# Attention into two expert layers: zero matmuls at the start, two weight loads and some small copies moved to other engines

## The chip, the cores and the metric

One core of one Trainium2 chip runs the program. It has TensorE (PE, with its weight loads as PEld), VectorE (DVE), ScalarE (ACT), GpSimd (POOL) and the sync engine (SP), which issues most DMAs. The metric is device time in microseconds, the median of several executions.

## The reference

Three stages follow each other on 2304 tokens (4 batches of 576) of width 512. The first is attention over a sliding window of 64 positions, 8 heads of 64. The second is a dense layer with a rational function between its two matrix products. The third sends each token to one of 8 experts.

```
scores = scale * q @ k.T ; mask: 0 <= row - col < 64, else -1e9
attn = exp(scores - max) ; attn /= sum(attn) + 1e-9 ; x = attn @ v
h = x @ w_in ; P = a0 + a1 h + a2 h^2 + a3 h^3
Q = 1 + |b0| |h| + |b1| h^2 ; y = (P / (Q + 1e-6)) @ w_out
e = argmax(y @ w_gate) ; weight = softmax(y @ w_gate)[e] * sigmoid(y @ w_output_gate)[e]
out = weight * (relu(y @ w1[e]) @ w2[e])
```

## The kernel before

Tokens go in 9 blocks of 256 (`TB`), and attention in 36 units: a block and a pair of heads each. For unit n, `at_T` transposes k and q on TensorE (line 308) and evacuates them to `kT` and the block-diagonal `qbd` (lines 157 to 163); from the second block on it first copies the last 64 columns of `kT` to its front (line 311 on GpSimd or 313 on VectorE, whichever is less charged). `at_QK` multiplies them into `sc`, takes the row minima of the negated, masked scores on VectorE (line 343), exponentials with row sums `sg` on ScalarE (349), adds 1e-9 to the sums on VectorE (352), takes reciprocals (353) and multiplies (`ms*sg`, line 173, on VectorE or GpSimd). `at_PT` transposes the weights, `at_PV` multiplies by v and splits the result into `xh` and `xl`.

q, k and v come through the sync queue in `load_qk` and `load_v`. For the first two blocks `load_v` loads each v row once and makes the shifted arrangement by three copies on chip (`copy`, line 167 on ScalarE or 169 on VectorE): one of 64 partitions and 512 numbers, two of 64 and 256.

The weights of the dense layer arrive as 64-bit floats. `load_w` loads a block of 1 MB, `convert` makes two fp32r halves of it: three integer operations of VectorE on each half block (288, 290, 292), a cast (167 or 169) and a subtraction (173). `c_conv(n)` starts conversions up to number n and issues the loads ahead of them.

The order of each engine's work is set when the kernel is built: the scheduler takes instructions by priority, which is program order shifted by `later(...)`, as its own timing model finds them ready, and each engine then runs its list in order. `evac`, `copy`, `arith` and `pick` give an operation to the engine whose charged load (`load`, by the formulas in `dve`, `act` and `pool`) would be lowest; `charge` adds the load of operations with a fixed engine. Ahead of the dense layer's first step, `PRE_E` = 12 half events of attention are emitted with `PRE_C` = 8 conversions among them, the first after `C_OFF` = 3 events; after that a step s emits the two products of one slice of 256 of the 2048 hidden columns, with attention and conversions paced beside it.

Of the kernel before, what the change touches and what calls it, by code (L numbers as in the profile page):

```python
# [1 line left out]

# [25 lines left out]
NG, HF = 3, 4  # L28
C_AT = ((-1, PRE_C), (6, 16), (15, 28), (18, 32))
A_OFF = 14  # L30
C_OFF, PREP = 3, 6
P_C, P_A, P_Y, P_L, P_E, P_G, P_S = -30, 0, -30, 0, 30, -30, 60
RK_R, G_LAG, F_LAG, F_LD, TR_S = 5, 3, 0, 1, 71

# [2 lines left out]
def kernel(  # L37
# [21 lines left out]
    W = 64  # L59
# [85 lines left out]
    def dve(n, fast=False):  # L145
        return 0.07 + n / (1920.0 if fast else 960.0)
# [84 lines left out]
    def load_v(m):  # L231
        u, g = divmod(m, 2)
        t = t4([128, 4, 4, D], "v")
        if u < VU:
            for x in range(2):
                for off, n, b, s in runs(u * TB + x * 128, 128):
                    nc.sync.dma_start(out=t[off:off + n, 2 * x + 1],
                                      in_=v[b, 4 * g:4 * g + 4, s:s + n, :].rearrange("h p d -> p h d"))
            copy(t[W:, 0:4:2], t[:W, 1:4:2], 8 * D)
            copy(t[:W, 2], t[W:, 1], 4 * D)  # L240
            copy(t[:W, 0], v_t[m - 2][W:, 3] if u else t[:W, 1], 4 * D)
            v_t[m] = t
            return
        for i in range(4):
            b, bi = divmod(4 * u + i, BPS)
            s0 = max(bi - 1, 0) * W
            n = W if bi == 0 else 2 * W
            nc.sync.dma_start(out=t[:n, i], in_=v[b, 4 * g:4 * g + 4, s0:s0 + n, :].rearrange("h p d -> p h d"))
        v_t[m] = t
# [6 lines left out]
    pos = {jf: s for s, jf in reversed(list(enumerate(seq)))}  # L256
    ffirst = [pos[0, fp] for fp in range(NFP)]

    def load_w(n):
        kind, fp = cseq[n]  # L260
        if kind == 0:
            t = t8([128, KD, 512], "stg", U32)
            src = w_in_u[:, fp * 512:(fp + 1) * 512]
        else:
            t = t8([128, 2, 1024], "stg", U32)
            src = w_out_u[fp * 256:(fp + 1) * 256, :]
        nc.sync.dma_start(out=t, in_=src.rearrange("(k p) f -> p k f", p=128))
        for i in range(2):
            r = t[:, 2 * i:2 * i + 2, :] if kind == 0 else t[:, i, :]
            stg[kind, fp, i] = (r[:, :, 0::2], r[:, :, 1::2]) if kind == 0 else (r[:, 0::2], r[:, 1::2])  # L270

    def convert(c):
# [7 lines left out]
        else:  # L280
            if i == 0:
# [3 lines left out]
        t = t2(shp, "ct")  # L285
        pu = pt(shp, "cp").bitcast(U32)
        charge("D", 2.0)
        nc.vector.tensor_scalar(out=pu, in0=hi, scalar1=3, scalar2=0x3FFFFFF8,
                                op0=ALU.logical_shift_left, op1=ALU.bitwise_and)
        nc.vector.scalar_tensor_tensor(out=pu, in0=hi, scalar=0xC0000000, in1=pu,  # L290
                                       op0=ALU.bitwise_and, op1=ALU.bitwise_or)
        nc.vector.scalar_tensor_tensor(out=t.bitcast(U32), in0=lo, scalar=29, in1=pu,
# [5 lines left out]


    P_t, pT_t, x_t = {}, {}, {}  # L300

    def at_T(n):
        u, c = divmod(n, NP)
        tq = pt([128, 2, 2, 128], "tq")
        cc = 2 * (c % 2)
        for a, src in ((0, k_t[n // 2]), (1, q_t[n // 2])):
            for r in range(2):
                nc.tensor.transpose(tq[:, a, r, :], src[:, r, cc:cc + 2, :].rearrange("p h d -> p (h d)"), ident)
        if u:
            if pick(D=dve(W, True), A=act(W), P=0.2) == "P":  # L310
                nc.gpsimd.tensor_copy(out=kT[c][:, :W], in_=kT[c][:, TB:])
            else:
                nc.vector.tensor_copy(out=kT[c][:, :W], in_=kT[c][:, TB:])
        evac(kT[c][:, W:], tq[:, 0].rearrange("d r p -> d (r p)"), TB)
        for hh in range(2):
            lo = 64 * hh
            evac(qbd[n % NQ][lo:lo + 64, :, lo:lo + 64],
                 tq[lo:lo + 64, 1].rearrange("d r (b p) -> d (r b) p", b=2), 256, -scale)
# [10 lines left out]
    def at_QK(n):  # L329
# [10 lines left out]
            nk.append(w)  # L340
        for i in range(4):
            charge("D", dve(128))
            nc.vector.tensor_tensor_reduce(
                out=ms[:, i, :nk[i]], in0=sc[:, i, :nk[i]], in1=cs[:, C_MASK + 128 - nk[i]:C_MASK + 128],
                scale=1.0, scalar=3.0e38, op0=ALU.add, op1=ALU.min, accum_out=mn[:, i:i + 1],
            )
        for i in range(4):
            charge("A", act(128))
            nc.scalar.activation(out=ms[:, i, :nk[i]], in_=ms[:, i, :nk[i]], func=AF.Exp,
                                 scale=-1.0, bias=mn[:, i:i + 1], accum_out=sg[:, i:i + 1])  # L350
        charge("D", 0.2)
        nc.vector.tensor_scalar(out=sg, in0=sg, scalar1=1e-9, scalar2=None, op0=ALU.add)
        nc.vector.reciprocal(out=sg, in_=sg)  # L353
        for a, b, w in spans(nk):
            arith(ms[:, a:b, :w], ms[:, a:b, :w], bc(sg[:, a:b], [128, b - a, w]), ALU.mult, (b - a) * w)
        P_t[n] = (ms, nk)

    def at_PT(n):
        ms, nk = P_t.pop(n)
# [514 lines left out]


    nc.vector.memset(one, 1.0)
    nc.scalar.preload_act_table_set("natural_log_exp_and_others")
    cseq.extend((kind, f0 + fp) for f0 in range(0, NFP, HF) for kind in range(2) for fp in range(HF))
    cpos = [0, 0]
# [78 lines left out]
    nc.sync.dma_start(out=cs, in_=cst[:, :C_TRI])  # L958
    v_upto(0)
    qk_upto(1)  # L960
    c_load(1)
    for t in qbd:
        nc.gpsimd.memset(t, 0.0)
    nc.scalar.activation(out=co[:, 4:6], in_=co[:, 4:6], func=AF.Abs)

    def prepare():
        wgs = t2([128, KD, 2 * E], "wgs")
# [52 lines left out]

    for n in range(TA):
        at_T(n)
    for i in range(PRE_E):
        at_upto(i + 1)
        c_conv(max(0, PRE_C * (i + 1 - C_OFF) // (PRE_E - C_OFF)))

    last = {j: s for s, (j, fp) in enumerate(seq) if fp == NFP - 1}
# [134 lines left out]
```

## Time and profile before

| | us |
|---|---|
| median of 3 runs | 808.82 (808.23 to 809.24) |
| the profiled execution | 810.46 |
| its span, first to last instruction | 808.5 |
| TensorE busy | 766.3 (95%) |
| VectorE busy | 539.0 (67%) |
| ScalarE busy | 506.3 (63%) |
| GpSimd busy | 449.9 (56%) |

Busy shares are means over stages that have different limits. Idle time counts where the engine that idles is the one that its stage waits for. A matmul's duration in a row is from issue to its modelled end, and the matmuls overlap; the busy time of a group, over its count, is the time from one to the next.

### The profile page before, as it was taken

Reading aid. Unit: us, or ns where it says so; the run is one execution under the profiler, and the core shown is the slowest. Engines: PE = TensorE matmul, PEld = TensorE weight load, DVE = VectorE, ACT = ScalarE, POOL = GpSimd, SP = SyncE. Lnnn points to the kernel's source line nnn. Section 1 sums busy time; section 2 is a strip of 40 time slices with the busy share of each in tenths; the row PEclk is TensorE's granted clock in tenths of the full one; section 3 lists DMA queues with packets and bytes.
Section 4 is the critical chain, followed back from the end, with each engine's and each line's share of the span. In section 5 each row is a group of like instructions: output and inputs, shape, how many; then the busy total and the mean of one; then the engine's idle time right before and its main releaser. Section 6 shows DMA issues by size and latency. Waiting matters only on the chain. (4 is left out here: it accounts for less than half of the span.)

```text
span 808.5 us, 15245 instructions
## 1 busy us (share of the span) xinstructions
PE 766.3 (95%) x5456; PEld 690.8 (85%) x5456; DVE 539.0 (67%) x1289; ACT 506.3 (63%) x1122; POOL 449.9 (56%) x399
## 2 busy tenths in 40 slices
PE   5868999999999999999999999897998999999994
PEld 4758899888899899999999998786997999999993
DVE  5799999876776766666676667465655456654630
ACT  5889786997766686676676665673525555543420
POOL 2596786665555555565654654675523554556430
PEclk9999999999999999999999999998998999999997
DMA  9786351422321211112120000323618777767610
GB/s 227 223 234 180 92 183 79 131 77 57 84 67 27 51 54 37 41 53 53 27 67 14 1 27 1 101 84 97 243 50 328 273 234 213 239 228 257 212 55 14
DMA packets 105602, 95.26 MB, mean 118 GB/s; under 512 B 77424, under 2 KB 77808, under 8 KB 105520
## 3 DMA queue, kind: packets, MB, share of 16 engines
q1 hardware_dynamic: 101840, 84.49, 35.1%
q0 software_dynamic: 3680, 9.73, 3.2%
q8 instruction: 45, 0.74, 0.4%
q14 instruction: 37, 0.30, 0.1%
HBM read 83.02 MB, written 11.44 MB: 117 GB/s over the span
## 5 line engine op out<-in xcount | busy, mean ns | idle before, releaser
L178 PE MATMUL y<-wo,g 128*128 128x512 f32 x864 | 220.1, 402 | 4.3 <-POOL g L173 3.3
L178 PE MATMUL h<-xh,wi 128*128 128x256 f32 x1024 | 195.8, 284 | 0.0
L178 PEld LDWEIGHTS y<-wo,g 128*128 128x128 f32 x864 | 158.4, 191 | 35.8 <-POOL g L173 3.5
L178 PEld LDWEIGHTS h<-xh,wi 128*128 128x128 f32 x1024 | 164.4, 192 | 2.7 <-DVE xl L388 0.2
L178 PE MATMUL h<-xl,wi 128*128 128x256 f32 x512 | 145.9, 285 | 0.0
L173 POOL TENSOR_TENSOR wx<-wr,wx 128x1024 fp32r<-128x1024 f32 x31 | 83.6, 2707 | 59.8 <-ACT wx L167 51.2
L173 POOL TENSOR_TENSOR g<-t,g 128x512 fp32r<-128x512 f32 x72 | 93.0, 1294 | 40.1 <-ACT g L167 34.8
L178 PE MATMUL hp<-xdh,wx 128*128 128x256 f32 x576 | 109.9, 290 | 3.8 <-ACT xdh L786 3.7
L173 POOL TENSOR_TENSOR qm<-qm,e 128x512 f32<-128x512 f32 x72 | 93.4, 1297 | 35.7 <-ACT qm L420 32.2
L178 PE MATMUL yp<-wx,hT 128*128 128x512 f32 x432 | 101.9, 392 | 0.0
L178 PEld LDWEIGHTS h<-xl,wi 128*128 128x128 f32 x512 | 98.3, 192 | 2.5
L178 PEld LDWEIGHTS hp<-xdh,wx 128*128 128x128 f32 x576 | 93.9, 198 | 5.3 <-ACT xdh L786 4.2
L415 ACT ACTIVATE e<-h 128x512 f32<-128x512 f32 x72 | 43.0, 597 | 87.3 <-PE h L178 87.1
L178 PEld LDWEIGHTS yp<-wx,hT 128*128 128x128 f32 x432 | 80.0, 188 | 16.4 <-DVE hT L794 0.3
L173 DVE TENSOR_TENSOR wx<-wr,wx 128x1024 fp32r<-128x1024 f32 x45 | 69.1, 1545 | 26.0 <-ACT wx L167 25.7
L167 ACT CAST wx<-wr 128x1024 fp32r<-128x1024 f32 x68 | 69.2, 1046 | 27.1 <-DMA wr<-in_moe_w_dram 21.8
L178 PE MATMUL hp<-xdl,wx 128*128 128x256 f32 x288 | 83.1, 290 | 0.7 <-DVE xdl L787 0.7
L440 DVE SCALAR_TENSOR_TENSOR t<-t,KK,r 128x512 f32<-128x512 f32 x72 | 53.6, 744 | 41.0 <-ACT r L434 40.6
L422 POOL TENSOR_SCALAR qm<-e,KK 128x512 f32<-128x512 f32 x45 | 34.6, 768 | 49.4 <-ACT e L415 49.2
L426 DVE TENSOR_TENSOR t<-t,h 128x512 f32<-128x512 f32 x72 | 49.1, 681 | 17.1 <-ACT t L416 17.0
L173 POOL TENSOR_TENSOR ms<-ms,sg 128x512 f32<-128x512 f32 (+4 forms) x60 | 39.2, 669 | 37.0 <-DVE sg L353 19.7
L433 ACT ACTIVATE r<-qm,KK 128x512 f32<-128x512 f32 x72 | 49.5, 688 | 15.3 <-POOL qm L173 14.7
(169 smaller groups left out, 1399.3 us busy)
## 6 DMA issues: line engine op xcount, KB each, us to landing
wr<-in_moe_w_dram SPq DMA_DIRECT2D x80, 512.0 KB, 4.8
stg<-in_moe_w_in_dram SPq DMA_DIRECT2D x8, 1024.0 KB, 6.7
stg<-in_moe_w_out_dram SPq DMA_DIRECT2D x8, 1024.0 KB, 7.4
v<-in_v_dram SPq DMA_DIRECT2D x58, 128.0 KB, 2.8
q<-in_q_dram SPq DMA_DIRECT2D x32, 128.0 KB, 2.8
k<-in_k_dram SPq DMA_DIRECT2D x32, 128.0 KB, 2.9
y_dram<-ysb SPq DMA_DIRECT2D x12, 256.0 KB, 2.1
yp_dram<-yq SPq DMA_DIRECT2D x6, 256.0 KB, 2.6
```

The costliest lines, as they stand in the source:

```text
L167: nc.scalar.copy(out=o, in_=i)
L173: (nc.vector if e == "D" else nc.gpsimd).tensor_tensor(out=o, in0=a, in1=b, op=op)
L178: pe[0] = nc.tensor.matmul(o, lhsT, rhs, start=start, stop=stop).ins
L415: nc.scalar.activation(out=e, in_=h, func=AF.Abs)
L422: (nc.vector if ef == "D" else nc.gpsimd).tensor_scalar(out=qm, in0=e, scalar1=co[:, 5:6], scalar2=co[:, 4:5], op0=ALU.mult, op1=ALU.add)
L426: nc.vector.tensor_tensor(out=t1, in0=t1, in1=h, op=ALU.mult)
L433: nc.scalar.activation(out=r0, in_=qm_t[s], func=AF.Ln, bias=qc_col)
L440: nc.vector.scalar_tensor_tensor(out=t1, in0=t1, scalar=co[:, 0:1], in1=r0, op0=ALU.add, op1=ALU.mult)
```

## The change

`at_T` and the start: a tile `wz` of zeros is set by VectorE, and `warm(n)` multiplies it n times by `one` into a PSUM tile that nothing reads: ten times at the start, six times behind the transposes of unit 1, six times behind those of the newest unit when four events are emitted. The first two weight blocks are loaded in two halves each by ScalarE's queue, behind its first activation (`Abs`), instead of by the sync queue. `C_OFF` becomes 0, and the first operation of each of the first four conversions is kept behind the newest unit's last row minimum on VectorE. The three copies in `load_v`, the `kT` copy in `at_T` and the addition of 1e-9 to `sg` are put on GpSimd, with loads charged for them.

```diff
--- before.py
+++ after.py
@@ -1,4 +1,4 @@
-from contextlib import ExitStack, contextmanager
+from contextlib import ExitStack, contextmanager, nullcontext
 
 import concourse.bass as bass
 import concourse.tile as tile
@@ -28,7 +28,7 @@
 NG, HF = 3, 4
 C_AT = ((-1, PRE_C), (6, 16), (15, 28), (18, 32))
 A_OFF = 14
-C_OFF, PREP = 3, 6
+C_OFF, PREP = 0, 6
 P_C, P_A, P_Y, P_L, P_E, P_G, P_S = -30, 0, -30, 0, 30, -30, 60
 RK_R, G_LAG, F_LAG, F_LD, TR_S = 5, 3, 0, 1, 71
 
@@ -236,9 +236,10 @@
                 for off, n, b, s in runs(u * TB + x * 128, 128):
                     nc.sync.dma_start(out=t[off:off + n, 2 * x + 1],
                                       in_=v[b, 4 * g:4 * g + 4, s:s + n, :].rearrange("h p d -> p h d"))
-            copy(t[W:, 0:4:2], t[:W, 1:4:2], 8 * D)
-            copy(t[:W, 2], t[W:, 1], 4 * D)
-            copy(t[:W, 0], v_t[m - 2][W:, 3] if u else t[:W, 1], 4 * D)
+            for o, i in ((t[:W, 0], v_t[m - 2][W:, 3] if u else t[:W, 1]), (t[W:, 0:4:2], t[:W, 1:4:2]),
+                         (t[:W, 2], t[W:, 1])):
+                charge("P", 0.6)
+                nc.gpsimd.tensor_copy(out=o, in_=i)
             v_t[m] = t
             return
         for i in range(4):
@@ -256,7 +257,7 @@
     pos = {jf: s for s, jf in reversed(list(enumerate(seq)))}
     ffirst = [pos[0, fp] for fp in range(NFP)]
 
-    def load_w(n):
+    def load_w(n, eng=None):
         kind, fp = cseq[n]
         if kind == 0:
             t = t8([128, KD, 512], "stg", U32)
@@ -264,7 +265,13 @@
         else:
             t = t8([128, 2, 1024], "stg", U32)
             src = w_out_u[fp * 256:(fp + 1) * 256, :]
-        nc.sync.dma_start(out=t, in_=src.rearrange("(k p) f -> p k f", p=128))
+        src = src.rearrange("(k p) f -> p k f", p=128)
+        if eng is None:
+            nc.sync.dma_start(out=t, in_=src)
+        else:
+            h = t.shape[1] // 2
+            for i in range(2):
+                eng.dma_start(out=t[:, i * h:(i + 1) * h], in_=src[:, i * h:(i + 1) * h])
         for i in range(2):
             r = t[:, 2 * i:2 * i + 2, :] if kind == 0 else t[:, i, :]
             stg[kind, fp, i] = (r[:, :, 0::2], r[:, :, 1::2]) if kind == 0 else (r[:, 0::2], r[:, 1::2])
@@ -285,8 +292,9 @@
         t = t2(shp, "ct")
         pu = pt(shp, "cp").bitcast(U32)
         charge("D", 2.0)
-        nc.vector.tensor_scalar(out=pu, in0=hi, scalar1=3, scalar2=0x3FFFFFF8,
-                                op0=ALU.logical_shift_left, op1=ALU.bitwise_and)
+        with tc.issue_after(dl[0]) if cpos[1] < 4 else nullcontext():
+            nc.vector.tensor_scalar(out=pu, in0=hi, scalar1=3, scalar2=0x3FFFFFF8,
+                                    op0=ALU.logical_shift_left, op1=ALU.bitwise_and)
         nc.vector.scalar_tensor_tensor(out=pu, in0=hi, scalar=0xC0000000, in1=pu,
                                        op0=ALU.bitwise_and, op1=ALU.bitwise_or)
         nc.vector.scalar_tensor_tensor(out=t.bitcast(U32), in0=lo, scalar=29, in1=pu,
@@ -298,6 +306,7 @@
 
 
     P_t, pT_t, x_t = {}, {}, {}
+    pl, dl = [None], [None]
 
     def at_T(n):
         u, c = divmod(n, NP)
@@ -305,12 +314,10 @@
         cc = 2 * (c % 2)
         for a, src in ((0, k_t[n // 2]), (1, q_t[n // 2])):
             for r in range(2):
-                nc.tensor.transpose(tq[:, a, r, :], src[:, r, cc:cc + 2, :].rearrange("p h d -> p (h d)"), ident)
+                pl[0] = nc.tensor.transpose(tq[:, a, r, :], src[:, r, cc:cc + 2, :].rearrange("p h d -> p (h d)"), ident).ins
         if u:
-            if pick(D=dve(W, True), A=act(W), P=0.2) == "P":
-                nc.gpsimd.tensor_copy(out=kT[c][:, :W], in_=kT[c][:, TB:])
-            else:
-                nc.vector.tensor_copy(out=kT[c][:, :W], in_=kT[c][:, TB:])
+            charge("P", 0.25)
+            nc.gpsimd.tensor_copy(out=kT[c][:, :W], in_=kT[c][:, TB:])
         evac(kT[c][:, W:], tq[:, 0].rearrange("d r p -> d (r p)"), TB)
         for hh in range(2):
             lo = 64 * hh
@@ -340,20 +347,27 @@
             nk.append(w)
         for i in range(4):
             charge("D", dve(128))
-            nc.vector.tensor_tensor_reduce(
+            dl[0] = nc.vector.tensor_tensor_reduce(
                 out=ms[:, i, :nk[i]], in0=sc[:, i, :nk[i]], in1=cs[:, C_MASK + 128 - nk[i]:C_MASK + 128],
                 scale=1.0, scalar=3.0e38, op0=ALU.add, op1=ALU.min, accum_out=mn[:, i:i + 1],
-            )
+            ).ins
         for i in range(4):
             charge("A", act(128))
             nc.scalar.activation(out=ms[:, i, :nk[i]], in_=ms[:, i, :nk[i]], func=AF.Exp,
                                  scale=-1.0, bias=mn[:, i:i + 1], accum_out=sg[:, i:i + 1])
-        charge("D", 0.2)
-        nc.vector.tensor_scalar(out=sg, in0=sg, scalar1=1e-9, scalar2=None, op0=ALU.add)
+        charge("D", 0.1)
+        charge("P", 0.15)
+        nc.gpsimd.tensor_scalar(out=sg, in0=sg, scalar1=1e-9, scalar2=None, op0=ALU.add)
         nc.vector.reciprocal(out=sg, in_=sg)
         for a, b, w in spans(nk):
             arith(ms[:, a:b, :w], ms[:, a:b, :w], bc(sg[:, a:b], [128, b - a, w]), ALU.mult, (b - a) * w)
         P_t[n] = (ms, nk)
+
+    def warm(n, after=None):
+        wu = pt([128, 512], "wu")
+        with tc.issue_after(after) if after else nullcontext():
+            for _ in range(n):
+                nc.tensor.matmul(wu, one, wz, start=True, stop=True)
 
     def at_PT(n):
         ms, nk = P_t.pop(n)
@@ -874,6 +888,9 @@
 
 
     nc.vector.memset(one, 1.0)
+    wz = t2([128, 512], "wz", BF16)
+    nc.vector.memset(wz, 0.0)
+    warm(10)
     nc.scalar.preload_act_table_set("natural_log_exp_and_others")
     cseq.extend((kind, f0 + fp) for f0 in range(0, NFP, HF) for kind in range(2) for fp in range(HF))
     cpos = [0, 0]
@@ -958,10 +975,13 @@
     nc.sync.dma_start(out=cs, in_=cst[:, :C_TRI])
     v_upto(0)
     qk_upto(1)
-    c_load(1)
     for t in qbd:
         nc.gpsimd.memset(t, 0.0)
-    nc.scalar.activation(out=co[:, 4:6], in_=co[:, 4:6], func=AF.Abs)
+
+    with tc.issue_after(nc.scalar.activation(out=co[:, 4:6], in_=co[:, 4:6], func=AF.Abs).ins):
+        for n in range(2):
+            load_w(n, nc.scalar)
+    cpos[0] = 2
 
     def prepare():
         wgs = t2([128, KD, 2 * E], "wgs")
@@ -1020,8 +1040,11 @@
 
     for n in range(TA):
         at_T(n)
+    warm(6, pl[0])
     for i in range(PRE_E):
         at_upto(i + 1)
+        if i == 3:
+            warm(6, pl[0])
         c_conv(max(0, PRE_C * (i + 1 - C_OFF) // (PRE_E - C_OFF)))
 
     last = {j: s for s, (j, fp) in enumerate(seq) if fp == NFP - 1}
```

## Rows read from the trace of the kernel before

**Rows 1.** Windows: stretch, us, each engine's busy us (instructions), clock, DMA share, GB/s.
```profile
5.44:28.00 22.56, 17.27 (x116) 14.90 (x117) 13.78 (x60) 16.75 (x60) 7.19 (x14) 0.92 1.11 271
28.00:80.00 52.00, 42.67 (x394) 37.91 (x393) 49.37 (x152) 45.95 (x146) 37.46 (x45) 0.97 0.75 204
80.00:400.00 320.00, 319.03 (x2397) 288.62 (x2396) 242.60 (x629) 234.63 (x565) 195.26 (x191) 1.00 0.25 70
```

**Rows 2.** Waits of VectorE, 5 to 28 us: us in total, times, longest.
```profile
DVE sg L352 <- ACT ms L349: 4.4, 2, 2.4
...
DVE ms L343 <- PE sc L178: 2.0, 2, 1.5
```

**Rows 3.** Windows of the transposes alone (line 308).
```profile
5.40:8.00 2.60, 1.98 (x8) 1.43 (x8) 1.00 1.11 225
21.90:23.10 1.20, 1.09 (x8) 0.86 (x8) 1.00 1.05 391
```

**Rows 4.** Timeline of TensorE: start, us, line, operation, count [idle before, what ended it].
```profile
5.47 0.91 PE L308 MATMUL tq<-KK,k 128*128 128x128 f32 x3 [5.47 <-DMA KK<-in_const_dram]
...
9.19 3.79 PE L178 MATMUL sc<-KK 128*128 128x64 f32 x16 [1.73 <-ACT KK L163]
12.77 0.85 PE L308 MATMUL tq<-KK,k 128*128 128x128 f32 x3
...
16.81 1.16 PE L178 MATMUL sc<-KK 128*128 128x64 f32 x8 [0.36 <-DVE KK L159]
...
26.62 1.95 PE L178 MATMUL sc<-KK 128*128 128x128 f32 x16
```

**Rows 5.** Windows of busy time with the granted clock, 18 to 21.5 us.
```profile
18.00:21.50 3.50, 3.50 (x21) 2.87 (x21) 2.06 (x10) 3.38 (x11) 0.69 (x1) 0.51 1.05 354
```

**Rows 6.** The page's groups: busy us, mean ns of one.
```profile
L178 PE MATMUL y<-wo,g 128*128 128x512 f32 x864 | 220.1, 402 | 4.3 <-POOL g L173 3.3
```

**Rows 7.** Groups of instructions of ScalarE, 0 to 84 us: busy us, mean ns.
```profile
L167 ACT COPY v<-v 64x256 f32<-64x256 f32 (+1 forms) x8 | 3.9, 483 | 0.2
```

**Rows 8.** Timeline of ScalarE.
```profile
7.28 0.37 ACT L161 COPY KK<-tq 128x256 f32<-128x256 f32 x1 [2.48 <-PE tq L308]
...
16.06 1.86 ACT L167 COPY v<-v 64x256 f32<-64x256 f32 x4
...
18.36 1.68 ACT L167 COPY v<-v 64x512 f32<-64x512 f32 x3
```

**Rows 9.** Groups of instructions of VectorE, 0 to 84 us.
```profile
L352 DVE TENSOR_SCALAR sg<-sg 128x4 f32<-128x4 f32 x12 | 3.3, 276 | 5.4 <-ACT ms L349 5.3
...
L313 DVE COPY KK<-KK 128x64 f32<-128x64 f32 x2 | 1.4, 680 | 1.3 <-PE sc L178 1.3
L169 DVE COPY v<-v 64x256 f32<-64x256 f32 (+1 forms) x4 | 1.3, 320 | 2.1 <-DMA v<-in_v_dram 2.0
```

**Rows 10.** Groups of instructions of GpSimd, 0 to 84 us.
```profile
L173 POOL TENSOR_TENSOR wi<-ct,wi 128x512 fp32r<-128x512 f32 x8 | 10.2, 1286 | 6.3 <-ACT wi L167 5.9 <-DVE wi L169 0.4
...
L422 POOL TENSOR_SCALAR qm<-e,KK 128x512 f32<-128x512 f32 x6 | 4.6, 770 | 0.0
...
L311 POOL COPY KK<-KK 128x64 f32<-128x64 f32 x11 | 2.7, 254 | 9.7 <-ACT KK L161 8.6 <-PE sc L178 0.8 <-DVE KK L157 0.3
```

**Rows 11.** Timeline of the DMA issues of the sync queue.
```profile
5.76 1.20 SPq L267 DMA_DIRECT2D stg<-in_moe_w_in_dram  x1
...
15.98 1.13 SPq L267 DMA_DIRECT2D stg<-in_moe_w_in_dram  x2
...
24.96 0.51 SPq L267 DMA_DIRECT2D stg<-in_moe_w_in_dram  x1
```

**Rows 12.** DMA queues, 0 to 40 us: packets by size.
```profile
DMA packets 17105, 9.08 MB, mean 227 GB/s; under 512 B 14669, under 2 KB 14797, under 8 KB 17101
```

**Rows 13.** Windows of busy time, clock, DMA share and GB/s.
```profile
9.00:11.50 2.50, 2.31 (x11) 2.31 (x12) 0.95 (x6) 0.14 (x1) 0.00 (x0) 1.00 1.06 371
11.50:18.00 6.50, 4.67 (x26) 4.09 (x26) 5.78 (x28) 5.71 (x23) 1.99 (x6) 1.00 1.35 227
```

## The prediction

> **What bounds the kernel now.** I read the busy time by stretch first. From 80 to 400 us TensorE is busy 319.0 of 320 us [rows 1]: nothing in this change makes its work there shorter, so a gain made before carries through to the end and a loss does too. The stages behind it have no line of the diff in them. What can be won lies ahead of 80 us. There the stretches differ. From 5.44 us, just ahead of the first transpose, to 28 TensorE idles 22.56 - 17.27 = 5.3 us, VectorE 8.8, ScalarE 5.8, GpSimd 15.4, and the DMA engines are full (share 1.11). From 28 to 80 us VectorE is busy 49.37 of 52, ScalarE 45.95, and TensorE idles 9.3: VectorE is what the stage waits for [rows 1]. So the start is worth as much as it lets VectorE begin its unbroken work earlier, plus what leaves VectorE altogether, and no more than TensorE's 5.3 + 9.3 = 14.6 us.
>
> The waits of VectorE come next: 4.4 us in two pieces, each before the small add on `sg`, each ended by an exponential on ScalarE; and 2.0 us before the row minima, ended by the score matmuls [rows 2]. The instructions behind the add on VectorE's queue (reciprocal, conversions) stand while it waits. So before 28 us the chain runs transposes, evacuations, scores, minima, exponentials, and ScalarE, not VectorE, ends most of the waits.
>
> **Zero matmuls.** Eight transposes, those of units 0 and 1, keep TensorE busy for 1.98 us, and eight later ones for 1.09 [rows 3]; sixteen score matmuls take 3.79 us at 9.19 and 1.95 us at 26.62 [rows 4]. The granted clock reads 0.51 in 18 to 21.5 us [rows 5] and 1.00 in 21.9 to 23.1 [rows 3], that is 1.2 and 2.4 GHz. Before 18 us it reads 1.00 as well, but the durations at 5 to 13 us are twice those at 22 to 28, so I go by the durations. With the upper level from the start, the transposes save 0.9 us, and the half of the scores that the first minima wait for (8 of 16) saves 0.9. Sum 1.8. Cost: ten zero matmuls of 512 columns, for which the nearest row is that of `y`, also of 512, 220.1 / 864 = 0.25 us each at the upper level [rows 6], so up to 0.51 at the lower. They start behind two memsets of VectorE, by my estimate at 1.4 us, and end by 6.5 at the latest. The first transpose started at 5.47 [rows 4], so it comes 0 to 1.0 late; I take 0.3, since the zeros, unlike `y`, do not change their weights. The two groups of six are at most 1.5 us each at the upper level; the scores at 9.19 had TensorE idle for 1.73 us before them [rows 4], which covers the first; were that cover gone, the scores would be 1.5 late. The second goes behind the transposes of unit 3, where inputs of the next scores are still being evacuated; I take nothing, 1.5 as the bound. Net +1.5, between 0 (the clock does not rise in time, and the zeros end late) and 1.8.
>
> **Small copies.** Twelve copies of v leave: eight from ScalarE, 483 ns each, 3.9 us [rows 7], seven of them in two blocks of 1.86 and 1.68 us at 16.06 and 18.36, in the stretch whose exponentials VectorE then waits for [rows 8]; and four from VectorE, 1.3 us [rows 9]. I count ScalarE's 3.9 in full at the front. On GpSimd the twelve have no row: its copy of 64 elements took 254 ns, its one-input pass over 512 elements 770 [rows 10], so 3.0 to 9.2 us in all; with four copies of 512 elements and eight of 256 I take 6. GpSimd idles 15.4 us before 28 [rows 1], which hides them; without that cover the products `ms*sg` behind them are late by up to 0.8 each. The add on `sg` leaves VectorE: twelve in the first 84 us at 276 ns, 3.3 us, and two kT copies at 680 ns, 1.4 us [rows 9]. But the reciprocal stays on VectorE and now waits for GpSimd, where the add stands behind whatever runs, up to 1.29 us [rows 10]. What is behind it on VectorE (minima, conversions, t) waits too. Between 0 and 12 x 1.29 = 15; the scheduler places the reciprocal where it expects the add to be done, so I take 0.1 each, 1.2 us.
>
> One part gives back. The planner's loads are charged 12 x 0.6 + 12 x 0.15 = 9 us more for GpSimd, and each 512-element operation that is therefore picked for VectorE instead of GpSimd closes 1.40 + 0.60 = 2.0 us of it: four or five operations come to VectorE, at about 0.6 us each, 2.7 us. VectorE after 28 us: 3.3 + 1.4 - 1.2 - 2.7 = +0.8, and I take +0.4, since a third or so of these operations lie before 28.
>
> **Weight loads by ScalarE.** Four issues of half a weight block follow the Abs, which ends 2.48 us ahead of the first evacuation at 7.28 [rows 8], at 4.80. On the sync queue a block took 1.20 us to issue at 5.76 and 0.51 at 24.96 [rows 11]. At 0.51 ScalarE is through at 6.8, at 1.20 at 9.6. The first evacuation would now be at about 6.7 (0.9 earlier, 0.3 later), so 0.1 to 2.9 us stick out. I take 0.7: two halves move what one block moved. The data is the larger matter. Of 17105 packets in the first 40 us 14669 are under 512 B [rows 12]: those are q, k and v, in rows of 64 numbers (256 B), and the weights come in rows of 512 (2 KB). The DMA moves 371 GB/s from 9 to 11.5 us and 227 from 11.5 to 18, at a share above 1 both times [rows 13]: the first I read as weights, the second as q, k and v. The second block (1 MB), issued at 15.98 before [rows 11], now goes ahead of most of k, q and v of the next units: 1 MB at 371 GB/s is 2.8 us of delay for them at the most, 0 at the least if the sync queue keeps its share. The first block went ahead of a part of them before as well. The scores of unit 2 began at 16.81, 4.0 us after their first transposes at 12.77 [rows 4], so a part of the delay is met by slack that is there; I take 1.0.
>
> The Trainium skill, "DMA: Bandwidth & Descriptors", section "Issuing engines are not separate DMA queues", says that transfers of all issuing engines share the same 16 engines and that a second issuer saves only issue time; by it alone this part gains no bandwidth and the sum loses nothing but these 0.7 + 1.0. The same page, "Queues, rings and completion order", has each engine go round robin between queues by packet, which with 2 KB against 256 B would favour the weights; this is the rival of late data below. No run here shows it yet, as before has one such queue.
>
> **Conversions.** The first four start behind the newest minima instead of between those of units 0 and 1, and eight are spread over twelve events instead of nine. The work is the same; with the second block there by about 13 us it can go into the 4.4 us in which VectorE waited for ScalarE. As those waits shrink by the parts above, I count nothing more for it, and keep 4.4 as what the best case adds.
>
> **Sum.** 1.5 (clock) + 3.9 (v copies off ScalarE) - 0.7 (issues) - 1.0 (later data) + 0.4 (VectorE after 28 us) = 4.1, and 0.3 off for the zeros' buffer and the longer `sg` chain in units 0 to 3: 3.8 us. The profiled execution took 810.46, with a span of 808.5; the median of the runs is 808.82. I take the 3.8 from the median: **805.0 us**.
>
> **Rivals.** *The front is swallowed (no change).* VectorE, ScalarE and GpSimd share 28 to 80 us by a planner that fills whichever is least charged; the sum of work does not fall, and GpSimd's copies are slower than those they replace. For it: VectorE at 95% there; against it: the three idle 30 us together before 28. If only 1 us of the 3.8 lasts: 807.8. *Late data (slower).* The weights win over q, k and v in the DMA engines, units 2 to 5 are transposed later, and GpSimd stands at a copy whose v has not landed, with all products behind it. It decides when the scores of unit 2 come after 16.8 + 3.8, that is past 20.6 us, which needs their q and k some 4 us before that, at 16.6 or later. For it: the share of 1.11 from 5.44 to 28 us [rows 1] and the short packets; against it: the 4.0 us between transposes and scores. With 2.8 us for data and 2.9 for the issues against a gain of 1.5 + 3.9 + 0.4 = 5.8 nothing is left, and a GpSimd that stands, with the reciprocals of two units behind it, adds 2 x 1.29 = 2.6: 811.3. *All gaps filled (faster by more).* The conversions take the 4.4 us of waits as well: 805.0 - 4.4 = 800.6, if VectorE then stays ahead. *The clock does not rise before the transposes:* the 1.5 is lost, 806.5, inside the forecast's own range.
>
> **How the numbers follow.** Forecast with the clock's case, 803 to 807.2: 0.50. More than that: 0.14. Swallowed: 0.21. Late data, or GpSimd's `sg` stall: 0.15. About 0.2% (1.6 us) is what a measurement of this kernel tells from none. Faster 0.64, same 0.21, slower 0.15. The range leaves out about half of the best and half of the worst case: 801.0 to 811.0; the forecast's own is 803 to 807.2.
>
> **What would show it.** In the changed profile: transposes at about 5.7 us with some 0.27 us each, the first sixteen score matmuls done by some 11.3 us instead of 12.98, no v copies on ScalarE, the 4.4 us in which VectorE waited for exponentials halved, TensorE idling some 11 instead of 14.6 us ahead of 80. The prediction is wrong if ScalarE's issues last past 9 us, if the transposes of unit 2 start after 16.6, if VectorE idles before the reciprocal, or if TensorE's idle time from 28 to 80 us stays at 9.

## The result, and the profile after

The changed kernel takes 814.31 us (median of 20 runs) beside 808.4 for the kernel before: a ratio of 1.0065, 95% interval 1.0053 to 1.0076. It is slower by 0.65%, outside the predicted range of 801.0 to 811.0. The span of its profiled execution is 812.0 us, before 808.5.

The windows of the changed kernel, columns as in [rows 1]:

```profile
5.44:28.00 22.56, 15.90 (x112) 12.09 (x112) 14.06 (x48) 12.17 (x44) 10.71 (x23) 0.82 1.12 281
28.00:80.00 52.00, 43.63 (x366) 38.81 (x365) 41.43 (x130) 46.33 (x143) 32.47 (x45) 0.82 0.60 168
80.00:400.00 320.00, 317.56 (x2352) 284.75 (x2352) 236.96 (x597) 238.14 (x579) 194.26 (x217) 1.00 0.27 74
400.00:600.00 200.00, 197.36 (x1399) 177.52 (x1398) 134.16 (x329) 126.30 (x250) 106.14 (x89) 1.00 0.21 67
```

Read the second row first. VectorE is busy 41.43 us where it was 49.37, and nothing comes of it: TensorE got through 366 matmuls instead of 394, and needed 43.63 us for them, at a mean clock of 0.82 instead of 0.97. So a part of the 8 us is no relief; less was done in the stretch. ScalarE is no freer, GpSimd does 5 us less. VectorE now idles 10.6 of 52 us. Its waits from 5 to 28 us (first two lines) and from 28 to 80 us (third), beside [rows 2]:

```profile
DVE ms L350 <- PE sc L178: 4.8, 2, 3.6
DVE KK L157 <- PE tq L317: 3.4, 1, 3.4
...
DVE sg L361 <- POOL sg L360: 6.6, 6, 1.9
```

The wait for exponentials ahead of the add is gone from VectorE; in its place the reciprocal waits for the add, on GpSimd. How TensorE starts, beside [rows 4]:

```profile
1.32 4.42 PE L370 MATMUL wu<-wz,KK 128*128 128x512 bf16 x10 [1.32 <-DVE KK L624]
5.62 0.76 PE L317 MATMUL tq<-KK,k 128*128 128x128 f32 x3
...
6.77 1.46 PE L370 MATMUL wu<-wz,KK 128*128 128x512 bf16 x6
8.47 2.05 PE L178 MATMUL sc<-KK 128*128 128x64 f32 x16 [0.24 <-ACT KK L163]
14.39 0.66 PE L317 MATMUL tq<-KK,k 128*128 128x128 f32 x2 [3.88 <-DMA k<-in_k_dram]
...
17.59 0.48 PE L317 MATMUL tq<-KK,k 128*128 128x128 f32 x1
...
21.01 1.95 PE L178 MATMUL sc<-KK 128*128 128x64 f32 x16
```

The first sixteen scores are done at 10.5 instead of 13.0 us, but the second sixteen begin at 21.01 instead of 16.81: their k and q are late. The sync queue's issues, and the `k` tiles from issue to landing (5 to 20 us; the longest, 8.3, is the one issued at 5.95):

```profile
5.95 0.37 SPq L226 DMA_DIRECT2D k<-in_k_dram  x1
...
10.04 0.37 SPq L226 DMA_DIRECT2D k<-in_k_dram  x1
...
DMA to landing us min/median/max: 5.8/6.0/8.3
```

And the clock, in three stretches of the changed kernel; before there were two of 3.4 us, one of them [rows 5]:

```profile
13.10:20.00 6.90, 4.95 (x30) 3.83 (x32) 3.60 (x12) 4.43 (x16) 4.74 (x8) 0.52 1.24 266
26.80:33.60 6.80, 6.56 (x30) 6.20 (x31) 6.27 (x32) 4.36 (x15) 3.87 (x6) 0.51 0.80 300
64.30:78.00 13.70, 11.04 (x83) 9.41 (x83) 10.13 (x25) 13.59 (x42) 6.88 (x13) 0.51 0.52 135
```

By this record TensorE is at 1.2 GHz for 27 us of the first 80, four times as long as before. The clock fell where TensorE idled: 3.88 us before 14.39, 0.97 + 0.87 between 23 and 27, 2.82 before 64.82, with two shorter waits behind that:

```profile
64.82 2.13 PE L178 MATMUL xp<-ms,v 128*64 128x64 f32 x32 [2.82 <-ACT ms L161]
...
69.50 1.09 PE L377 MATMUL pp<-KK,ms 128*128 128x128 f32 x4 [1.49 <-DVE xl L402]
71.23 1.51 PE L178 MATMUL xp<-ms,v 128*64 128x64 f32 x16 [0.65 <-ACT ms L161]
```

At the other end something came back that the prediction had not in view. The page's group of `y`, beside [rows 6]:

```profile
L178 PE MATMUL y<-wo,g 128*128 128x512 f32 x864 | 216.8, 397 | 0.7 <-DVE ct L300 0.3
```

The wait of 3.3 us for GpSimd's `g` is gone. It stood at 558 us, in the dense layer's last step. The first fence has three lines of GpSimd and TensorE before, the second a line each of GpSimd, VectorE and TensorE after:

```profile
556.11 0.97 POOL L596 DMA_INDIRECT t_dram<-KK,rk  x1 [3.81 <-ACT g L167]
557.11 2.50 POOL L173 TENSOR_TENSOR g<-t,g 128x512 fp32r<-128x512 f32 x2
558.43 3.78 PE L178 MATMUL y<-wo,g 128*128 128x512 f32 x8 [3.33 <-POOL g L173]
```

```profile
563.78 1.31 POOL L173 TENSOR_TENSOR g<-t,g 128x512 fp32r<-128x512 f32 x1
...
565.04 0.68 DVE L173 TENSOR_TENSOR g<-t,g 128x512 fp32r<-128x512 f32 x1
...
566.86 3.36 PE L178 MATMUL y<-wo,g 128*128 128x512 f32 x14
```

Before, all 72 products for `g` are GpSimd's; after, the planner gives one, the last, to VectorE. The wait cost more than its 3.3 us, since the clock fell during it (eighth column, before):

```profile
555.00:560.00 5.00, 1.68 (x5) 1.28 (x5) 0.92 (x3) 1.66 (x2) 3.47 (x3) 0.73 0.76 238
560.00:565.00 5.00, 5.00 (x21) 4.39 (x20) 1.24 (x2) 2.10 (x2) 2.38 (x1) 0.59 0.30 73
```

The eight `y` matmuls behind it took 3.78 us, fourteen in the changed kernel 3.36.

To compare runs I use one number worked out from the traces: how late TensorE is. Its matmuls are added up with the mean cost that each shape has from 90 to 500 us of the kernel before, zeros left out; "late at 100" says how many us after before's 100 us the same sum is reached. The table has that, the us at 1.2 GHz from 5 to 127 us by the clock record, what VectorE's reciprocal or add waited for GpSimd (5 to 84 us), and the `y<-POOL g` wait.

```
                      ratio [95%]              late at 100  500  780   1.2 GHz  sg wait  y wait
after                 1.0065 [1.0053,1.0076]      7.0  10.4   3.3    27.3     7.8    none
e1  no ACT loads      1.0035 [1.0017,1.0053]      6.2   4.0   2.6    20.5     3.2    none
e2  ACT loads alone   1.0123 [1.0084,1.0161]      7.7   6.1   6.9    17.1     -      3.5
e3  no zeros          1.0066 [1.0041,1.0092]     11.1   9.5   2.8    23.9     0.4    none
e4  no GpSimd moves   0.9965 [0.9942,0.9987]     -0.6  -1.4  -4.7     6.8     -      3.7
e5  sg back           1.0051 [1.0032,1.0070]      8.3   6.7   0.6    27.3     -      3.6
e6  v back            0.9927 [0.9905,0.9949]      1.6   0.8  -8.3    13.7     1.4    none
e7  old charges       1.0177 [1.0143,1.0210]     17.6  15.7  12.9    30.7     1.3    3.3
e8  zeros, conv alone 1.0060 [1.0039,1.0080]      7.2   5.1   3.1    27.3     -      3.3
e9  before nudged     1.0032 [1.0015,1.0049]     -1.5   1.4   2.1    10.2     -      3.6
e10 after nudged      1.0013 [0.9996,1.0030]      9.5   7.6  -3.4    23.9     3.1    none
e11 v back, nudged    0.9903 [0.9873,0.9934]      0.7  -0.1  -9.9    13.7     1.3    none
e12 v moved alone     1.0049 [1.0013,1.0084]      6.5   5.3   8.0    13.7     -      3.7
e13 dummy copies      1.0056 [1.0028,1.0083]     10.2   9.2   4.3    23.9     5.2    none
e14 v not charged     0.9980 [0.9954,1.0006]      3.1   6.4  -0.4    13.7     3.6    none
e15 v, block 1        0.9910 [0.9878,0.9942]      1.3   1.1  -4.1    13.7     2.0    none
e16 v, block 2        0.9967 [0.9950,0.9984]      6.9   5.4  -2.0    13.7     2.9    none
e17 zeros at 60 us    0.9990 [0.9964,1.0017]      6.3   4.7  -2.6    13.7     4.0    none
e18 v back, no zeros  0.9999 [0.9978,1.0020]      4.1   2.1  -3.6     3.4     0.8    none
```

So the changed kernel is 7.0 us late at 100, 10.4 at 500, and has 3.3 of it left at the end; the spans differ by 3.5. All columns but the ratio come from one execution of each kernel. The one of e12 took 4.6 us more than the kernel's median, those of e15 and before 2.8 and 2.1 more, those of e3 and e10 3.3 less, and 20 executions of the kernel before lie between 807.09 and 814.09: a us or two in the column "780" is not a difference between kernels.

The same sum at other times tells two things more. The front is not lost where the copies run (7 to 24 us). At 64 us the changed kernel is 1.8 us late, at 70, behind the wait of 2.82 us above, it is 8.0, and at 80 7.4. And between 552 and 566 us, across the place of the `y` wait, it wins 6.4 us on the kernel before, and the eleven others without that wait win 3.7 to 6.7; the seven that have it win 1.0 at the most. So the lost wait, with the slow stretch behind it, gave back about as much as the front had lost by 80 us, and a kernel with the wait is compared with one without it at 500 us, not at the end.

### The profile page after: what moved, and what is told of

Same layout as the page of the kernel before. It is cut to its first block, busy times and chain, and to the rows that moved or that the text cites. A ratio compares the mean times of both kernels' runs of the same rounds, so it can differ in the third digit from the quotient of the medians.

```text
span 812.0 us, 15320 instructions
## 1 busy us (share of the span) xinstructions
PE 773.9 (95%) x5477; PEld 690.9 (85%) x5478; DVE 544.1 (67%) x1241; ACT 508.6 (63%) x1129; POOL 449.7 (55%) x441
## 5 line engine op out<-in xcount | busy, mean ns | idle before, releaser
L178 PE MATMUL y<-wo,g 128*128 128x512 f32 x864 | 216.8, 397 | 0.7 <-DVE ct L300 0.3
L178 PE MATMUL h<-xh,wi 128*128 128x256 f32 x1024 | 198.0, 286 | 1.3 <-ACT KK L163 1.3
L178 PE MATMUL yp<-wx,hT 128*128 128x512 f32 x432 | 104.5, 397 | 4.2 <-ACT hT L807 2.1
L173 POOL TENSOR_TENSOR qm<-qm,e 128x512 f32<-128x512 f32 x70 | 90.6, 1294 | 31.6 <-ACT qm L434 28.3
L178 PE MATMUL hp<-xdh,wx 128*128 128x256 f32 x576 | 105.7, 283 | 1.5 <-ACT xdh L800 1.5
L178 PEld LDWEIGHTS hp<-xdh,wx 128*128 128x128 f32 x576 | 90.6, 192 | 2.5 <-ACT xdh L800 2.0
L173 DVE TENSOR_TENSOR wx<-wr,wx 128x1024 fp32r<-128x1024 f32 x45 | 76.4, 1713 | 19.4 <-ACT wx L167 19.1
L167 ACT CAST wx<-wr 128x1024 fp32r<-128x1024 f32 x63 | 64.4, 1048 | 27.1 <-DMA wr<-in_moe_w_dram 22.3
L356 ACT ACTIVATE ms<-ms,mn 128x128 f32<-128x128 f32 (+1 forms) x144 | 55.6, 390 | 5.6 <-DVE mn L350 5.5
L821 POOL DMA_INDIRECT out_dram<-ob,tl x19 | 21.6, 1138 | 62.3 <-ACT ob L163 31.9
```

The costliest lines, as they stand in the source:

```text
L167: nc.scalar.copy(out=o, in_=i)
L173: (nc.vector if e == "D" else nc.gpsimd).tensor_tensor(out=o, in0=a, in1=b, op=op)
L178: pe[0] = nc.tensor.matmul(o, lhsT, rhs, start=start, stop=stop).ins
L821: nc.gpsimd.indirect_dma_start(out=out, out_offset=bass.IndirectOffsetOnAxis(ap=tl[:, hh, 0:1], axis=0), in_=ob, in_offset=None, bounds_ch ...
```

## The experiments

Each was run against the kernel before; ratios are in the table.

**One part undone.** e1 puts the weights back on the sync queue:

```diff
-    with tc.issue_after(nc.scalar.activation(...).ins):
-        for n in range(2):
-            load_w(n, nc.scalar)
-    cpos[0] = 2
+    c_load(1)        # in its old place, behind qk_upto(1)
```

> The changed kernel with the first weight block back on the sync queue, issued where the kernel before issues it, and the second issued by the pacing. Late data (the weights on ScalarE's queue hold back q and k of units 2 and 3): the first transposes of unit 2 come at 12 to 13 us instead of 14.4 and the last of that pair by 14 instead of 18, and the time falls by 4 us or more, to 810 or below. GpSimd theory (the add on sg and the copies there hold up VectorE): the time stays at 813 to 815.

812.45 us, within what a mere reordering does (e9 to e11, below). The data are early here: the scores of unit 2 begin at 13.44 us.

```profile
13.44 1.16 PE L178 MATMUL sc<-KK 128*128 128x64 f32 x8
```

TensorE is still 6.2 us late at 100: the late k and q alone are not the loss.

e3 takes out `wz` and all three `warm` calls.

> The changed kernel without the zero matmuls. If they bring what the sum said (1.5 us) the time is 815 to 816; if the clock they raise is lost again in the starved stretch behind, 813 to 815, no difference; if they cost (they stand in TensorE's queue behind late transposes) 812 or below.

816.51 us, the same ratio as the change. In this kernel the zeros bring nothing that lasts: without them it is 11.1 instead of 7.0 late at 100, but even at the end.

e4 takes all of GpSimd's new work back (v and kT copies, the add):

```diff
-                charge("P", 0.6)
-                nc.gpsimd.tensor_copy(out=o, in_=i)
+            copy(t[W:, 0:4:2], t[:W, 1:4:2], 8 * D)    # and the two others; kT by pick(); sg by nc.vector
```

> The changed kernel with the v and kT copies and the add on sg where before has them. GpSimd theory: 810 or below. Late data: transposes of unit 2 as late as in the changed kernel (14 to 18 us), and 813 or more, since ScalarE has 3.9 us of copies again.

807.28 us, faster than before. The moves to GpSimd cost 1.0%; e5 and e6 split them. e5 returns only the add on `sg` to VectorE, e6 only the three `copy` calls of v.

> The changed kernel with only the addition of 1e-9 to sg back on VectorE (charges as before for it). If the wait of the reciprocal on GpSimd (7.8 us in the first 84 us of the changed kernel) is what the GpSimd part costs: 807 to 810. If it is the v copies or the planner's charges: 812 to 815.

811.77 us: the add is not what costs most, although VectorE's longest new wait is for it. It is not shown to be free either, for the `y` wait is back in this kernel: at 500 us it is 6.7 late where the change is 10.4, 3.7 less (the nudge of e10, below, moves 2.8 there).

> The changed kernel with only the v copies back on ScalarE and VectorE. If the v copies in GpSimd's queue, which wait for late v with the adds on sg behind them, are the cost: 807 to 810. If the add on sg is: 812 to 816, as ScalarE has 3.9 us more.

802.47 us: the copies are, together with the load charged for them. Undoing them alone is worth 1.4%, some 11 us, and the rest of the change is 0.7% faster than before. That gain is not made in the front: at 500 us e6 is 0.8 late, and from 552 to 566 us it wins 6.7 on before. The same stretch of e6, and two lines of its waits and of TensorE's timeline:

```profile
28.00:80.00 52.00, 45.51 (x395) 40.93 (x396) 46.80 (x148) 47.69 (x152) 41.90 (x58) 0.90 0.70 193
```

```profile
DVE sg L360 <- POOL sg L359: 1.4, 2, 0.8
```

```profile
15.90 0.66 PE L316 MATMUL tq<-KK,k 128*128 128x128 f32 x2 [5.05 <-DMA k<-in_k_dram]
...
22.57 2.05 PE L178 MATMUL sc<-KK 128*128 128x64 f32 x16 [1.07 <-ACT KK L163]
```

GpSimd works 41.90 us there instead of 32.47, and VectorE waits for it 1.4 instead of 6.6. The scores of unit 2 come even later than in the changed kernel, 22.57, in a kernel that beats both. At 64 us e6 is later than the change, 3.4 against 1.8; at 80 it is 1.1 late, the change 7.4.

**One part alone.** e2 is before with the two weight loads on ScalarE's queue.

> The kernel before with the two weight loads on ScalarE's queue and nothing else. Late data: the transposes of unit 2 end at 16 us or later instead of 14.7, and the time is 811 or more. GpSimd theory: within 1 us of before, 808 to 809.

819.31 us. e8 is before with the zero matmuls and the conversions' new order, weights on the sync queue.

> The kernel before with the zero matmuls and the conversion order alone; weights on the sync queue, all small operations where before has them. Late data and GpSimd theories together: both costs are gone, 803 to 806, the lowest of all so far. Reordering theory (every variant lands anywhere within 5 us): no better than the 807.3 of the variant without the GpSimd part.

813.39 us. Each alone loses (+1.2 and +0.6%); together, in e4, they gain 0.35%. In e8 the conversions are due from the first event on, while the second block is still issued late by the sync queue; in e2 the blocks are early and nothing takes them up. That is how I read it; only the three ratios are shown.

e7 is the change with the planner charged as before the change, that is, told nothing of the moves:

```diff
-            charge("P", 0.25)
+            pick(D=dve(W, True), A=act(W), P=0.2)    # likewise three picks per v block, and 0.2 on D for sg
```

> The changed kernel with all its moved operations on GpSimd, but the planner's loads charged as before charges them, so that the other operations go to the engines to which they would go without the move. If the cost is in the operations themselves (waits): 812 to 816. If it is that the charges send products to VectorE: 807 to 810.

823.31 us, the slowest of all, 1.1% above the change: here charges that do not fit the work cost more than the moves.

**The same kernels in another order.** A load of 0.04 more for VectorE at each add on `sg` changes no work, but hundreds of places in the order:

```diff
-        charge("D", 0.2)
+        charge("D", 0.24)        # in the changed kernels 0.1 becomes 0.14
```

> Before, with the load that the planner charges VectorE for the sg addition raised from 0.20 to 0.24; the work is the same, but some operations go to another engine and TensorE's order differs in 904 lines. Theory A (the change has its effect through queues and data at the start): within 2.5 us of before, 806 to 811. Theory B (any nudge of the planner reorders the whole attention stage and moves the time by as much as the change did): 4 us or more away from 808.4, on either side.

811.07 us.

> After, with the same nudge: 0.10 to 0.14 for VectorE's part of the sg addition. Theory A: 811.5 to 817, and slower than before nudged the same way by 3 us or more. Theory B: anywhere from 804 to 822; the difference to before nudged the same way may have either sign.

810.15 us.

> After with the v copies back on ScalarE and VectorE, which took 802.5, with the same nudge of 0.04. Theory A (the v copies at the head of GpSimd's queue are what costs): 800 to 805, and 8 us or more below the nudged after. Theory B: the 802.5 was one lucky order, the nudged one comes out at 806 to 812.

800.82 us. The nudge moves the three kernels by +0.3, -0.5 and -0.2%. So a difference of half a per cent between two orders is not yet a cause, and that holds for the change itself: nudged, it and before are 0.2% apart, with the change ahead. The cost of the v copies is above that: 1.4% without the nudge, 1.1% with it.

**What of the copies costs.** e12 is before with the v copies alone moved.

> Before with the twelve v copies alone on GpSimd; weights on the sync queue, no zero matmuls, sg on VectorE. Theory A: GpSimd waits for v's data 3 us or more at the head of its queue, and what it owes to VectorE and TensorE is late: 811 to 816. Without the late data of the two ScalarE loads the copies would be hidden, as the prediction had it: 803 to 807, ScalarE's 3.9 us won. Theory B: no telling, 4 us to either side.

814.26 us, 6.5 us late at 100: as late as the whole change.

e13 leaves the copies where they were and gives GpSimd twelve others:

```diff
+            for hh in (2, 1, 1):      # at the end of the first two load_v blocks; dz: a constant tile of zeros
+                charge("P", 0.6)
+                nc.gpsimd.tensor_copy(out=dz[:W, :hh * 256], in_=dz[W:, :hh * 256])
```

> After with the v copies back on ScalarE and VectorE (802.5 so far), plus twelve GpSimd copies of the same sizes, charged 0.6 each as in the change, that read and write a tile of zeros nobody else uses: GpSimd's time and the planner's charge without the wait for v's data. If time or charge is what costs: TensorE 6 us or more late at 100 us and 808 to 814. If the wait for the data and what stands behind it costs: within 3 us of 802.5.

814.4 us. From its groups of GpSimd (0 to 84 us) and its window:

```profile
L246 POOL COPY dz<-dz 64x256 f32<-64x256 f32 (+1 forms) x12 | 5.6, 467 | 0.7
```

```profile
28.00:80.00 52.00, 41.23 (x344) 36.72 (x345) 39.96 (x129) 45.41 (x144) 35.04 (x52) 0.83 0.59 168
```

The dummies wait for no data and feed nobody, and cost what the copies cost. So it is not v's landing: it is GpSimd's time, or the charge. And the 3.9 us that the change saves on ScalarE bring nothing that can be seen, since this kernel does not save them and takes the same time within 0.3%.

e14 is the change without `charge("P", 0.6)`; the copies stay on GpSimd.

> After, with the 0.6 that the planner charges GpSimd for each v copy left out (7.2 in all); the copies are still on GpSimd. If the charge costs (it sends products to VectorE): 803 to 808. If the copies themselves cost: 811 to 818, and not earlier at 100 us than after, which was 7.0 late there.

809.14 us: 0.85 of the 1.4 points go with the charge. The 0.5 that are left to the copies themselves are no more than a mere reordering moves. GpSimd is busy 37.8 us from 28 to 80 again (32.5 in the change), and none of the products for `ms` goes to VectorE (three in the change).

e15 and e16 move the copies of the first or of the second token block only:

```diff
+                if u == 0:                       # e16: u == 1
+                    charge("P", 0.6)
+                    nc.gpsimd.tensor_copy(out=o, in_=i)
+                else:
+                    copy(o, i, n)
```

> After, with only the six copies of the first token block on GpSimd, which run at 7 to 10 us in a GpSimd that has nothing else. They are hidden by every theory: 800 to 805. If they are not, the data wait at the head of the queue isn't the cause.

803.42 us: hidden, but not because GpSimd had nothing else. Only three of the six copies ran at 7 to 9 us; the other three ran at 16.97 to 18.79, behind an add and two products, and cost nothing there:

```profile
7.10 0.84 POOL L243 COPY v<-v 64x256 f32<-64x256 f32 x2 [3.15 <-DMA v<-in_v_dram]
...
8.48 0.60 POOL L243 COPY v<-v 64x512 f32<-64x512 f32 x1
...
15.95 1.07 POOL L173 TENSOR_TENSOR ms<-ms,sg 128x64 f32<-128x64 f32 x2 [0.32 <-DVE sg L364]
16.97 0.84 POOL L243 COPY v<-v 64x256 f32<-64x256 f32 x2
...
18.18 0.61 POOL L243 COPY v<-v 64x512 f32<-64x512 f32 x1
```

> After, with only the six copies of the second token block on GpSimd, which run at 15 to 24 us between the sg additions and products of units 0 to 3. If GpSimd's wait for data and its queue there cost: all of the loss, 810 to 816, 5 us or more late at 100 us. If the loss is no single place: half of it, 806 to 809.

808.03 us, 6.9 us late at 100, where e15 is 1.3 late. One of its copies ran at 8.47 us, the other five at 19.55 to 22.50. The second block has all of the loss at 100 us, but only about 0.4 of the 1.4 points at the end, within what a reordering moves; and the two halves do not add up to the whole (-0.2 and +0.4 against +1.4, from e6). At 64 us the two kernels are even, 1.4 and 1.5 late; e16 loses its time from there to 80. So place in the queue is not shown to be what decides.

**The clock.** e17 adds zeros for the gap at 62 us:

```diff
+        if n == 9:
+            warm(12, pe[0])          # in at_QK, behind the score matmuls
```

> After, with twelve more zero matmuls behind the transposed weights of the unit before unit 9's scores, at about 60 us, where TensorE idled 2.8 us and the granted clock then read 0.50 from 64 to 78 us. If the clock is a cause: 1.00 in 62 to 78, 3 to 5 us of the 7.0 at 100 us back, 809 to 812. If the clock only follows from waits that come from other engines: the waits stay, the lower level moves elsewhere, and the 2.6 us of zeros are not won back: 813 to 818.

807.95 us, but not by that road. The zeros were placed behind another wait and did not fill the gap:

```profile
63.16 1.12 PE L178 MATMUL xp<-ms,v 128*64 128x64 f32 x16 [3.36 <-ACT ms L161]
...
67.74 3.24 PE L372 MATMUL wu<-wz,KK 128*128 128x512 bf16 x10 [0.22 <-issue]
```

TensorE is still 6.3 us late at 100, where 2 to 4 were expected; what it gains on the change it gains behind 100 us, where no zeros are. Inconclusive: whether the later stretches at 1.2 GHz are a cause or follow from the waits stays open. e14 and e16 have half of them, and 3.1 and 6.9 us of lateness.

e18 is e6 without the zeros.

> After with the v copies back on ScalarE and VectorE and without the 22 zero matmuls. The prediction's term for the clock at the start was 1.5 us in the zeros' favour: 803 to 805 against 802.5 with them, at the lower level until 13 us or later. If the early clock feeds nothing that is late: 799 to 802.5, as 7.4 us of matmuls are gone.

808.81 us, 0.7% above e6. The starts of e18 and of e6:

```profile
5.53 0.87 PE L316 MATMUL tq<-KK,k 128*128 128x128 f32 x3 [5.53 <-DMA KK<-in_const_dram]
...
9.06 3.78 PE L178 MATMUL sc<-KK 128*128 128x64 f32 x16 [1.60 <-ACT KK L163]
```

```profile
5.43 0.49 PE L316 MATMUL tq<-KK,k 128*128 128x128 f32 x3
...
8.80 2.05 PE L178 MATMUL sc<-KK 128*128 128x64 f32 x16 [1.04 <-ACT KK L163]
```

With zeros the sixteen scores end 2.0 us earlier; e6 is 2.5 us ahead of e18 at 100, 1.3 at 500 and 4.7 at 780. What it gains behind 500, where the zeros have no part, I put down to the order; that is not shown.

## Why the prediction was wrong

**The step that failed is "Small copies".** It credited 3.9 us for ScalarE and let GpSimd's 15.4 idle us before 28 hide the twelve copies. Their size was right, as this group shows (5.6 us; 6 taken), and so was the planner's answer in kind (three products to VectorE, 1.8 us; four or five and 2.7 us taken):

```profile
L242 POOL COPY v<-v 64x256 f32<-64x256 f32 (+1 forms) x12 | 5.6, 465 | 4.4 <-DMA v<-in_v_dram 3.8
```

The sign was wrong: moved, and charged for, the copies cost 9 to 11 us (after against e6, and the nudged pair) instead of bringing 3.9. Of the 1.4 points 0.85 went when the charge alone was left out (e14): the larger part is what the planner dealt out anew, a term that the prediction had at 2.7 us of VectorE's time and no more. The nearest rival, late data, has GpSimd stand at a copy whose v has not landed; it did so for 3.8 us, but e13's dummies wait for nothing and cost the same.

How the copies cost is not shown. ScalarE's time did not stay free: the planner fills whichever engine is least charged, and from 28 to 80 us ScalarE is as busy as before (46.33 and 45.95). GpSimd's queue before 28 us, which the prediction asked about, is not where the time went: at 64 us the change is less late than e6, and it loses its time from there to 80, in the wait for ScalarE's `ms` and at 1.2 GHz behind it. e2 and e8, with the copies in their old place, lose 6.2 and 5.8 us in the same 16 us. Why some orders fall badly there and others do not stays open.

Without the credit of 3.9 the sum comes to -0.1 us, and that is what the front of the kernels without these copies shows: e6 is 0.8 late at 500 us, its nudged twin 0.1 early. That is a sum of terms of which some were wrong, as follows, so I take the agreement for luck. Of the signs of being wrong that the prediction named, two came: VectorE idles before the reciprocal, and TensorE's idle time from 28 to 80 us hardly fell, 8.4 from 9.3; from 5.44 to 80 it is 15.0 where 11 was forecast.

**"0.1 us each" for the reciprocals was too little.** The group over 0 to 84 us:

```profile
L361 DVE RECIPROCAL sg<-sg 128x4 f32<-128x4 f32 x11 | 1.9, 176 | 7.9 <-POOL sg L360 7.8
```

7.8 us against 1.2 taken and 15 as the bound. But e5, without that wait, and e3, with 0.4 us of it, are later still at 100 us, so the wait is not the loss there.

**"VectorE is what the stage waits for" did not hold when VectorE was relieved.** It was 95% busy there [rows 1]; in the changed kernel it is 80% busy, and the stage is longer. I read that as a chain over four engines, of which a busy share names the fullest, not the one whose relief shortens the chain; no run tests it alone.

**Later data: the event came, its price did not.** The rival's condition was met, scores past 20.6 us (21.01; q landed at 16.5, a little ahead of the 16.6 named), against 1.0 us of delay taken. Yet e6, with scores at 22.57, is the fast kernel, and e1, with scores at 13.44, still loses. The Trainium skill, "DMA: Bandwidth & Descriptors", "Queues, rings and completion order", has each DMA engine go round robin between queues by packet. The 8.3 us of a `k` tile beside the weights agree with that: in the kernel before, where both stood in one queue, the `k` tile issued ahead of the block took 3.7 and the one issued behind it 5.8. No run here separates it from the 16 engines being full.

**The clock at the start: right in kind, its size open.** Eight transposes in 1.31 us instead of 1.98 [rows 3], first minima at 9.66 instead of 11.30. The 1.5 predicted are 2.5 at 100 us in e18 against e6 and 4.1 in e3 against the change; at the end they are 0.7% in the one pair and nothing in the other. What was left out is that the level falls again at later waits, three times before 80 us. ScalarE's four issues took 2.09 us, 0.52 each, and the first evacuation came at 7.11: right too.

```profile
4.98 2.09 ACTq L274 DMA_DIRECT2D stg<-in_moe_w_in_dram  x4
7.11 0.37 ACT L161 COPY KK<-tq 128x256 f32<-128x256 f32 x1 [1.93 <-PE tq L317]
```

**"The stages behind it have no line of the diff in them" was false.** The add on `sg` runs in all 36 units, and its charge (0.1 less on VectorE, 0.15 more on GpSimd) sways the planner to the end. The 3.3 to 3.7 us before the last `y` stand in all eight kernels with the add on VectorE or the old charges, and in none of the other twelve, where one to three `g` products go to VectorE. That gave back 6.4 of the 10.4 us that the change was late at 500: that it lost only 0.65% is luck, of a kind that the prediction did not count on. e6, 1.6 us late at 100 us, owes its whole gain to what lies behind 500, 6.7 us of it to this wait.

Not settled: why the kernels drift by up to 3.4 us against before between 100 and 500, either way; what of the 1.4 to 11.0 us that these twelve kernels regain behind 500 is not that one wait; and how much of either is more than the order they fell into, or than one execution differs from the next.

## What to carry to other kernels

Where a planner fills engines by charged load, a move is not local: it changes everything emitted after it, and the time that leaves one engine is not its worth, even where the other engine idles for longer. Here twelve copies, 5.6 us in all, on an engine that idled 15.4 us in that stretch, cost 9 to 11, and more than half of that went with the load charged for them. Nudge a charge in both kernels before a difference of half a per cent is called an effect. Ask at which us the lateness arises before naming its cause: here it was 40 us behind the last of the copies. Look at the waits of later stages as well as at the place of the edit: one wait of 3.3 us, with the slower clock behind it, was worth more than all that the front was forecast to win. Undo the parts one at a time: here a change that lost 0.65% held one that wins 0.7 to 1.0%, all of it but the v copies.

## What the runs showed of the hardware that was not expected

- An add over 128x4 took 221 ns on GpSimd, in the changed kernel, and 276 on VectorE [rows 9]: for a few elements per partition GpSimd was not the slower engine.

```profile
L360 POOL TENSOR_SCALAR sg<-sg 128x4 f32<-128x4 f32 x11 | 2.4, 221 | 10.5 <-ACT ms L356 7.3 <-DMA k<-in_k_dram 1.9 <-DMA v<-in_v_dram 1.0
```

- A 128 KB load in 256 B rows, issued among four half blocks of 512 KB in 2 KB rows on another queue, landed after 8.3 us. With the block in the same queue, one such load issued ahead of it took 3.7 us and one behind it 5.8.
- TensorE's clock fell to 1.2 GHz after an idle time of 2.8 us at 62 us, in the middle of the run, and stayed there for 13.7 us, 11.0 of them busy, with two more waits of 1.5 and 0.65 us inside.
- Near the end of the dense layer of the kernel before it fell during a wait of 3.3 us and stayed low for 6.8, so that this wait was worth about 6.4 us, not 3.3.
